# Attention and a gated feed-forward on one core: seven products joined in PSUM through a ScalarE copy, weights converted in pairs of chunks

## The chip, the core and the metric

The kernel runs on one NeuronCore of a Trainium2 chip. The metric is the device time of one execution, in microseconds (us), and lower is better. Four engines compute: PE (TensorE, matmuls, with PEld loading its weights), DVE (VectorE), ACT (ScalarE) and POOL (GpSimd). SP (SyncE) only issues DMAs here. Matmul results land in PSUM, which has eight banks; everything else lies in SBUF.

## What is computed

The reference, cut to what matters (8 batches, 8 heads, 576 positions, head size 64; 4608 tokens, model width 512, hidden width 2048):

```python
q_s = softmax(q, axis=-1)            # over the 64 of a head
k_s = softmax(k, axis=2)             # over the 576 positions
kv  = einsum('bhsd,bhse->bhde', k_s, v)
x   = einsum('bhsd,bhde->bhse', q_s, kv)   # as (4608, 512)
h   = x @ w_in                       # 512 -> 2048
g   = h * (1 / (1 + exp(-1.702 * h)))
out = g @ w_out                      # 2048 -> 512
```

The weights arrive as 64-bit floats and are turned into 32-bit ones on the chip.

## The kernel before, in words

**Precision.** Every large matmul is done three times on halves: a number is split into a rounded high part and the rest (`h` and `l`), and high x high, high x low and low x high are added in one PSUM bank.

**Work.** Tokens come in 12 tiles of 384. Tiles 0 and 1 go through the plain feed-forward: `g1` multiplies x by one of 16 chunks of `w_in` (12 matmuls of 384 columns), ACT applies the gelu, `g2` multiplies by the chunk of `w_out` (three times 3 matmuls of 512 columns). Tiles 2 to 11 go in five pairs, and there the first feed-forward matmul is Winograd's form of Strassen's scheme: a 2 x 2 block product made of seven products in place of eight. A pair takes eight cycles `n` (40 in all); a cycle has seven `product`s, numbered 1, 6, 2, 7, 5, 4, 3 in their order in the list `PROD` (6 matmuls of 384 columns each), and six `out_part`s, called G below, of the cycle before (6 matmuls of 512 columns each, into banks 0 to 5). With p1 to p7 the products, the four results are p1+p2, p1+p6+p7+p4, p1+p6+p7+p5 and p1+p6+p5+p3 (signs lie in the operands).

**Where the sums are made.** Products use banks 6 and 7. Before, p2, p4 and p3 join a bank that already holds a product (`JOINS`); the other sums are additions of a bank and an SBUF tile by DVE, in `add`: five per cycle. ACT copies p1 out and applies the gelu (`finish`), rounds its result to the high part, and DVE subtracts to get the low part.

**Attention.** For each batch: maximum over positions (`k_max`, DVE and a POOL reduction), subtraction and exp (`k_sub`), 40 small matmul pairs (`kv_pairs`), division. For each tile: the softmax of q (`q_soft`), transposes on PE (`q_tr`), the product with kv (`x_pairs`), copies out of PSUM (`x_raw`), sums and splits of x (`t_make`, `x_split`). For batches 0 and 1 and tiles 0 to 3 heads come in fours, later in twos.

**Weights.** A chunk is loaded (`load_w`, 512 KB), converted by two ACT and four DVE instructions (`conv_w`: of 512 elements per partition), and stored back to DRAM (`store`), from where the 40 cycles refill slots of SBUF. `s_make` forms the four weight sums of a cycle.

**Order.** Nothing is scheduled by a compiler here. `Plan` collects every step with an engine, an estimated cost, the buffers it reads and writes and a rank; `Plan.order` lets each engine take, whenever it is free, the ready step of lowest rank, and the instructions are issued in that order. So each engine runs a fixed sequence, in order, with semaphores between engines. `FIRST` is a table of ranks that replaces the written ranks of all steps below rank 16. Exp and gelu need different ACT tables, so ACT reloads a table between them.

Of the kernel before, what the change touches and what calls it, by code (L numbers as in the profile page):

```python
# [18 lines left out]
class Plan:  # L19
# [80 lines left out]

FIRST = [
# [20 lines left out]
]  # L122

# [11 lines left out]
def efficient_attention_then_gelu_ffn(  # L135
# [24 lines left out]
    LAG = 2  # L160
    SM = 512
# [54 lines left out]
    def early(tag, name, shape, batch):  # L216
        held[tag] = batch
        return sb(name, shape, tag=tag), (tag, 0)

    ek, ev, eq, en, etail = {}, {}, {}, {}, {}  # L220
    for gr in range(2):
        ek[0, gr] = early(f"wi{5 + gr}", f"ek0{gr}", [P, 4, CM, D], 0)
        eq[0, gr] = early(f"wi{7 + gr}", f"eq0{gr}", [P, 4, C, D], 0)
        en[0, gr] = early(f"wo{7 + gr}", f"en0{gr}", [P, C, 4, D], 0)
        en[1, gr] = early(f"wo{10 + gr}", f"en1{gr}", [P, C, 4, D], 1)
        ev[0, gr] = early(f"w{'io'[gr]}9", f"ev0{gr}", [P, 4, CM, D], 0)
        ek[1, gr] = early(f"wo{14 + gr}", f"ek1{gr}", [P, 4, CM, D], 1)
        eq[1, gr] = early(f"wi{14 + gr}", f"eq1{gr}", [P, 4, C, D], 1)
        ev[1, gr] = early(f"wo{12 + gr}", f"ev1{gr}", [P, 4, CM, D], 1)
    em, _ = early("wi13", "em", [P, 4 * 4 * D], 1)  # L230
    emx = [em[:, y * 4 * D : (y + 1) * 4 * D].rearrange("p (h d) -> p h d", h=4) for y in range(2)]
    em1 = em[:, 2 * 4 * D :]
    et, _ = early("wi10", "et", [P, H * (D + W)], 0)
# [10 lines left out]
        for kind in ("wi", "wo", "sh", "sl")  # L244
# [5 lines left out]

    def load_w(j, kind, rank):
        tag = f"{kind}{j}"

        def run():
            raw = sb(f"raw", [P, 2 * DM], I32, tag=tag)
            raws[tag] = raw
            if kind == "wi":
                nc.sync.dma_start(
                    out=raw.rearrange("p (c f) -> p c f", c=KC),
                    in_=w_in[:, 2 * j * P : 2 * (j + 1) * P].rearrange("(c p) f -> p c f", p=P),  # L260
                )
            else:
                nc.sync.dma_start(out=raw, in_=w_out[j * P : (j + 1) * P, :])

        plan.add("SP", plan.ISSUE, (), ((tag, 0), (tag, "v")), rank, run, size=2 * DM * 4 * P)

    nt = [0]

    def next_tmp():
        nt[0] += 1  # L270
        return nt[0] % 3

    def conv_w(j, kind, rank):
# [5 lines left out]
        tag = f"{kind}{j}"  # L279
        i = next_tmp()  # L280
        ff = tmp[i]
        f = ff.bitcast(I32)

        def words():
            return raws[tag].rearrange("p (f t) -> p f t", t=2)
# [8 lines left out]
        def c3():  # L294
            w = words()
            nc.vector.scalar_tensor_tensor(f, f, 3, w[:, :, 0], ALU.logical_shift_left, ALU.bitwise_or)  # L296
            nc.vector.scalar_tensor_tensor(f, w[:, :, 1], -0x80000000, f, ALU.bitwise_and, ALU.bitwise_or)

        def c5():
            w = sb("w", [P, 2 * DM], F32R, tag=tag)  # L300
            nc.scalar.copy(w[:, :DM], ff)
            raws[tag] = w

        def c6():
            w = raws[tag]
            wh, wl = w[:, :DM], w[:, DM:]
            nc.vector.tensor_tensor(out=wl, in0=ff, in1=wh.bitcast(F32), op=ALU.subtract)
            dst = wi if kind == "wi" else wo
            dst[0][j], dst[1][j] = (
                x.rearrange("p (c f) -> p c f", c=KC) if kind == "wi" else x for x in (wh, wl)  # L310
            )
# [925 lines left out]
```

## Time and profile before

| | us |
|---|---|
| median of 3 runs (lowest, highest) | 900.97 (899.77, 901.08) |
| the profiled execution, whole | 897.6 |
| its span, first to last instruction | 895.8 |
| PE busy | 852.4 (95%) |
| DVE busy | 561.4 (63%) |
| ACT busy | 482.1 (54%) |

The share of PE is an average over very different stretches: the first 83.6 us, in which weights and the first attention are made, the stretch to 224 us, in which tiles 0 and 1 are finished and the cycles start, and the 40 cycles. Matmuls overlap in PE's pipeline, so a matmul's own duration is longer than the step from its start to the next one's start; the step is what counts.

### The profile page before, as it was taken

What the parts mean: (1) busy time and instruction counts of PE and PEld (TensorE: products, weight loads), DVE (VectorE), ACT (ScalarE), POOL (GpSimd) and SP (SyncE); (2) the same over time, 40 slices, a digit from 0 to 9 for tenths busy, and PEclk for the clock granted to TensorE, in tenths of its full rate; (3) what the DMA queues carried; (4) which work ended last, traced back from release to release, by engine and by line L of the source; (5) the groups of instructions that cost most, each with busy time, mean ns of one, the idle gap of its engine ahead of it and who ended that gap; (6) DMA issues with size and microseconds to landing.
All of it is one profiled execution on the core that took longest, in us unless ns stands there. A gap on an engine that the chain in (4) does not pass through costs nothing.

```text
span 895.8 us, 13356 instructions
## 1 busy us (share of the span) xinstructions
PE 852.4 (95%) x4960; PEld 744.4 (83%) x4960; DVE 561.4 (63%) x1090; ACT 482.1 (54%) x856; POOL 29.8 (3%) x35
## 2 busy tenths in 40 slices
PE   3779999898999999899999999999999999999998
PEld 3668988687888888788898888789888889898896
DVE  8989989987977756647646646646553346332332
ACT  3776668877676447656635545525643326332222
POOL 1100000020200000101000001000000000000000
PEclk9889999999999999999999999999999999999999
DMA  9999974268565558957556648736744545745341
GB/s 277 281 318 399 375 229 134 102 174 222 181 206 198 196 200 252 279 183 241 174 177 232 214 171 249 233 135 211 253 161 166 198 153 190 268 162 216 140 153 70
DMA packets 133184, 187.52 MB, mean 209 GB/s; under 512 B 65536, under 2 KB 96256, under 8 KB 133120
## 3 DMA queue, kind: packets, MB, share of 16 engines
q1 hardware_dynamic: 133120, 186.68, 62.6%
q8 instruction: 39, 0.64, 0.3%
q14 instruction: 25, 0.20, 0.1%
HBM read 152.04 MB, written 34.60 MB: 208 GB/s over the span
## 4 chain that ended last, share of the span: by engine, by line
PE 83%; DVE 8%; DMA 4%; ACT 2%; SPq 1%; issue 1%; DVEq 0%; ACTq 0%
PE bank L1013 35%; PE bank L942 30%; PE bank L699 6%; PE bank L731 6%; PE bank L525 2%; DMA qt<-in_q 2%; PE bank L675 2%; DVE g L958 1%; PE bank L608 1%; DMA ev<-in_v 1%; DVE qm L587 1%; PE bank L670 1%; DVE tmp L296 1%; DMA raw<-in_moe_w_out 1%; DMA out<-tmp 1%
## 5 line engine op out<-in xcount | busy, mean ns | idle before, releaser
L1013 PE MATMUL bank<-w,gp 128*128 128x512 f32 x954 | 254.4, 396 | 0.6 <-ACT gp L969 0.4
L1013 PEld LDWEIGHTS bank<-w,gp 128*128 128x128 f32 x954 | 176.2, 188 | 36.6 <-issue 3.8
L942 PE MATMUL bank<-xc,w 128*128 128x384 f32 x960 | 190.6, 338 | 6.5 <-DVE g L958 4.5
L958 DVE TENSOR_TENSOR g<-bank,g 128x384 f32<-128x384 f32 x200 | 110.9, 556 | 127.2 <-PE bank L942 118.7
L942 PEld LDWEIGHTS bank<-xc,w 128*128 128x128 f32 x960 | 170.0, 188 | 18.3 <-DVE g L958 6.9
L942 PE MATMUL bank<-w 128*128 128x384 f32 x720 | 141.3, 340 | 4.2 <-DVE g L958 4.1
L966 ACT ACTIVATE g<-g 128x384 f32<-128x384 f32 x120 | 63.1, 526 | 146.4 <-DVE g L958 146.1
L942 PEld LDWEIGHTS bank<-w 128*128 128x128 f32 x720 | 128.6, 189 | 11.9 <-DVE g L958 6.0
L972 DVE TENSOR_TENSOR gp<-g,gp 128x384 fp32r<-128x384 f32 x106 | 58.6, 556 | 85.5 <-ACT gp L969 84.3
L1013 PE MATMUL bank<-w,gh 128*128 128x512 f32 x324 | 103.3, 400 | 0.0
L699 PE MATMUL bank<-xh,w 128*128 128x384 f32 x256 | 73.8, 351 | 4.1 <-ACT g L705 2.6
L966 ACT ACTIVATE g<-bank 128x384 f32<-128x384 f32 x40 | 19.7, 492 | 98.0 <-PE bank L942 97.9
L1013 PEld LDWEIGHTS bank<-w,gh 128*128 128x128 f32 x324 | 59.3, 188 | 12.1 <-issue 3.2
L1013 PE MATMUL bank<-w,gl 128*128 128x512 f32 x162 | 63.9, 395 | 0.0
L731 PE MATMUL bank<-w,gh 128*128 128x512 f32 x192 | 62.5, 407 | 0.2 <-ACT gh L708 0.2
L969 ACT CAST gp<-g 128x384 fp32r<-128x384 f32 x106 | 54.6, 515 | 3.4
L972 DVE TENSOR_TENSOR gl<-g,gh 128x384 fp32r<-128x384 f32 x54 | 30.0, 556 | 41.5 <-ACT gh L969 40.6
L699 PEld LDWEIGHTS bank<-xh,w 128*128 128x128 f32 x256 | 48.7, 196 | 6.7 <-ACT g L705 3.3
L699 PE MATMUL bank<-xl,w 128*128 128x384 f32 x128 | 44.3, 346 | 0.0
L731 PEld LDWEIGHTS bank<-w,gh 128*128 128x128 f32 x192 | 35.6, 190 | 7.9 <-issue 1.2
L731 PE MATMUL bank<-w,gl 128*128 128x512 f32 x96 | 38.7, 403 | 2.4 <-DVE gl L711 2.4
L463 POOL PARTITION_ALL_REDUCE mx<-mx x24 | 23.9, 997 | 501.8 <-DVE mx L459 501.8
(123 smaller groups left out, 995.8 us busy)
## 6 DMA issues: line engine op xcount, KB each, us to landing
w<-dwo SPq DMA_DIRECT2D x80, 512.0 KB, 4.9
w<-dwi SPq DMA_DIRECT2D x44, 512.0 KB, 3.9
w<-dsh SPq DMA_DIRECT2D x32, 512.0 KB, 6.2
w<-dsl SPq DMA_DIRECT2D x32, 512.0 KB, 7.2
out<-tmp SPq DMA_DIRECT2D x36, 256.0 KB, 3.3
raw<-in_moe_w_out SPq DMA_DIRECT2D x16, 512.0 KB, 9.0
raw<-in_moe_w_in SPq DMA_DIRECT2D x16, 512.0 KB, 10.1
dwi<-w SPq DMA_DIRECT2D x16, 512.0 KB, 6.6
```

The costliest lines, as they stand in the source:

```text
L296: nc.vector.scalar_tensor_tensor(f, f, 3, w[:, :, 0], ALU.logical_shift_left, ALU.bitwise_or)
L463: nc.gpsimd.partition_all_reduce(flat, flat, P, bass_isa.ReduceOp.max)
L525: nc.tensor.matmul(pk[r0 : r0 + D, m, cols], lhs, rhs, start=c == 0, stop=c == CM, tile_position=(0, r0))
L675: nc.tensor.matmul(po[ro], kx[ri, ro], qx[ri], start=True, stop=True, tile_position=((a ^ odd) * D, a * D))
L699: nc.tensor.matmul(ph, wi[w][j][:, c, :], x[:, c, :], start=c == 0 and i == 0, stop=c == KC - 1 and i == 2,)
L731: nc.tensor.matmul(po[c], x[:, cs], wo[w][j], start=j == 0 and i == 0, stop=j == NJ - 1 and i == 2)
L942: nc.tensor.matmul(pb, ws[w][:, c * P : (c + 1) * P], xx[x][:, c * TB : (c + 1) * TB], start=p not in JOINS and c == 0 and i == 0, stop=c ...
L958: lambda: nc.vector.tensor_tensor(out=d, in0=pb, in1=o, op=ALU.add),
L966: lambda: nc.scalar.activation(d, src, AF.Gelu_apprx_sigmoid), table="gelu")
L969: plan.add("ACT", act(TB), (dk,), hk, early_, lambda: nc.scalar.copy(get()[0], d))
L972: lambda: nc.vector.tensor_tensor(out=get()[1], in0=d, in1=get()[0].bitcast(F32), op=ALU.subtract),
L1013: nc.tensor.matmul(po, x[:, cs], w[:, h * DM : (h + 1) * DM], start=m == 0 and e == 0 and i == 0, stop=m == NQ - 1 and e == 1 and i == 2,)
```

## The change

1. **Sums in PSUM.** After p1, ACT copies bank 6 into bank 7 (`keep`), and p6, p7 and p4 join bank 7, p2 joins bank 6, p3 joins p5 in bank 6; only p1 and p5 start a bank (`FRESH`). ACT copies bank 7 out after p6 and after p7. DVE keeps two additions per cycle of five. A matmul joins only where an earlier matmul has written the bank; after `x_pairs` has used bank 7 (`seeded`), one extra matmul of 384 columns into bank 7 goes ahead of p1.
2. **Cycle.** `CYCLE` has a new order of products and G, and two slots for attention; `q_tr` uses bank 6; the copies out of its bank, and all of `x_raw`, go to DVE for tiles 4 and later, and so does kv's division. `gate` makes ACT's attention exps wait for a point late in a cycle's products.
3. **Pairs of chunks.** Chunks 2 to 15 are loaded and converted two at a time, with instructions of 1024 elements. Four of the `w_in` sums are stored as they are converted (`dsr`) and loaded by `s_make`, instead of being added again.
4. **Fours.** Heads come in fours everywhere.
5. **Ranks.** `FIRST` covers every step below rank 48, and holds other numbers.

```diff
+LIMIT = 48
 FIRST = [
-    10880, -13523, -14348, -9747, -11942, -16592, -13346, -10333, -12197, -7632, -8889, -7141, -10712, -8175, -8834,
...
+    -7413, -6848, -6096, -5820, -6089, -6938, -5819, -4545, -5036, -4544, -4855, 7784, -5658, 8215, 7935, -5883,
...
-        plan.add("ACT", 0.66, (R,), (T,), rank, c1)
-        plan.add("DVE", 0.40, (R,), (R,), rank, c2)
-        plan.add("DVE", 1.36, (R, T), (T,), rank, c3)
-        plan.add("ACT", 0.62, (T,), (R,), rank, c5)
-        plan.add("DVE", 0.69, (R, T), ((tag, 1),), rank, c6)
+        T, R = ("work", i), [(tag, 0) for tag in tags]
+        m = n * DM
+        plan.add("ACT", 0.23 + m / 1190, R, (T,), rank, c1)
+        plan.add("DVE", 0.13 + m / 1900, R, R, rank, c2)
+        plan.add("DVE", 0.147 + m / 960, (*R, T), (T,), rank, c3)
+        plan.add("DVE", 0.147 + m / 960, (*R, T), (T,), rank, c4)
+        plan.add("ACT", act(m), (T,), R, rank, c5)
+        plan.add("DVE", 0.157 + m / 960, (*R, T), [(tag, 1) for tag in tags], rank, c6)
...
     def group(b):
-        return 4 if b < 2 else 2
+        return 4
...
-            nc.scalar.copy(qT, pq[:, :TB])
-
-        plan.add("ACT", act(TB), (PB,), (Q,), rank, run_c)
+            (nc.vector.tensor_copy if t >= EARLY_T else nc.scalar.copy)(qT, pq[:, :TB])
+
+        plan.add("DVE" if t >= EARLY_T else "ACT", act(TB), (PB,), (Q,), rank, run_c)
...
     BANK = {1: 6, 2: 6, 5: 6, 3: 6, 6: 7, 7: 7, 4: 7}
-    JOINS = (2, 4, 3)
+    FRESH = (1, 5)
...
+            if seed:
+                nc.tensor.matmul(bank[7][:, :TB], ws[0][:, :P], xx[0][:, :TB], start=True, stop=True)
...
-                        start=p not in JOINS and c == 0 and i == 0, stop=c == 1 and i == 2,
+                        start=p in FRESH and c == 0 and i == 0, stop=c == 1 and i == 2,
...
+        def keep(dst, key):
+            plan.add("ACT", act(TB), (PB,), (key,), early_, lambda: nc.scalar.copy(dst, pb))
+
         if p == 1:
-            st["p1"] = d, dk = temp()
-            plan.add("ACT", act(TB), (PB,), (dk,), early_, lambda: nc.scalar.copy(d, pb))
-        elif p == 6:
-            st["u2"] = temp()
-            add(st["u2"], st["p1"])
-        elif p == 2:
-            finish(pb, (PB,), temp(), 0, 0)
-        elif p == 7:
-            st["u3"] = temp()
-            add(st["u3"], st["u2"])
-        elif p == 5:
-            add(st["u3"], st["u3"])
-            finish(st["u3"][0], (st["u3"][1],), st["u3"], 1, 1)
-        elif p == 4:
-            c21 = temp()
-            add(c21, st["u2"])
-            finish(c21[0], (c21[1],), c21, 1, 0)
+            keep(bank[7][:, :TB], ("bank", 7))
+        elif p in (6, 7):
+            st[p] = temp()
+            keep(*st[p])
+        elif p in (2, 4):
+            finish(pb, (PB,), temp(), int(p == 4), 0)
         else:
-            c12 = temp()
-            add(c12, st["u2"])
-            finish(c12[0], (c12[1],), c12, 0, 1)
+            dst = st[7] if p == 5 else temp()
+            add(dst, st[7 if p == 5 else 6])
+            finish(dst[0], (dst[1],), dst, int(p == 5), 1)
...
-    CYCLE = [1, ("G", 0), 6, ("G", 1), 2, "early", ("G", 2), "wide", ("G", 3), 7, ("G", 4), 5, 4, ("G", 5), 3, "tail"]
+    CYCLE = [1, ("G", 0), 6, 2, ("G", 1), 7, 5, ("G", 2), 4, 3, ("G", 3), "slot0", ("G", 4), "slot1", ("G", 5)]
```

How the order of the instructions moves, at three places. First PE in a late cycle without attention. Lines L942 and L1102 are products (bank_69 and bank_70 are banks 6 and 7; `xc` and `w` are the slots of x, `xc` for products 1, 6, 2, 7), L1013 and L1167 are G. Before:

```order
L942 MATMUL bank_70<-xc,w 128x384 x6
L942 MATMUL bank_69<-xc,w 128x384 x6
L1013 MATMUL bank_63<-w,gp 128x512 x6
L1013 MATMUL bank_64<-w,gp 128x512 x6
L942 MATMUL bank_69<-xc,w 128x384 x6
L1013 MATMUL bank_65<-w,gp 128x512 x6
L1013 MATMUL bank_66<-w,gp 128x512 x6
L942 MATMUL bank_70<-xc,w 128x384 x6
L1013 MATMUL bank_67<-w,gp 128x512 x6
L942 MATMUL bank_69<-w 128x384 x6
L942 MATMUL bank_70<-w 128x384 x6
L1013 MATMUL bank_68<-w,gp 128x512 x6
```

And with the change:

```order
L1102 MATMUL bank_69<-xc,w 128x384 x6
L1167 MATMUL bank_63<-w,gp 128x512 x6
L1102 MATMUL bank_70<-xc,w 128x384 x6
L1102 MATMUL bank_69<-xc,w 128x384 x6
L1167 MATMUL bank_64<-w,gp 128x512 x6
L1102 MATMUL bank_70<-xc,w 128x384 x6
L1102 MATMUL bank_69<-w 128x384 x6
L1167 MATMUL bank_65<-w,gp 128x512 x6
L1102 MATMUL bank_70<-w 128x384 x6
L1102 MATMUL bank_69<-w 128x384 x6
```

Before, p6 stood ahead of p1 and two G stood between the first products; now p1 comes first, one G stands between it and p6, and three G follow p3.

Second, ACT in the same cycle, from the copy after p1 on. Before (L977 copies p1, L966 is the gelu, L969 the rounding):

```order
L977 COPY g_84<-bank_69 128x384
L966 ACTIVATE g_78<-bank_69 128x384
L969 CAST gp<-g_78 128x384
L966 ACTIVATE g_79<-g_79 128x384
L969 CAST gp<-g_79 128x384
L966 ACTIVATE g_80<-g_80 128x384
L969 CAST gp<-g_80 128x384
L966 ACTIVATE g_81<-g_81 128x384
L969 CAST gp<-g_81 128x384
```

And with the change (L1138 is `keep`):

```order
L1138 COPY bank_70<-bank_69 128x384
L1138 COPY work_83<-bank_70 128x384
L1127 ACTIVATE work_84<-bank_69 128x384
L1131 CAST gh_89<-work_84 128x384
L1138 COPY work_84<-bank_70 128x384
L1127 ACTIVATE work_84<-work_84 128x384
L1131 CAST gp<-work_84 128x384
L1127 ACTIVATE g_78<-bank_70 128x384
L1131 CAST gp<-g_78 128x384
L1127 ACTIVATE g_79<-g_79 128x384
L1131 CAST gp<-g_79 128x384
```

One copy of a cycle became three, and the first of them writes the bank that p6 joins.

Third, the head of SP's queue of DMAs. Before:

```order
L428 DMA eq_132<-in_q 128x4x192
L345 DMA et<-in_k 64x8x64
L360 DMA ek_131<-in_k 128x4x256
L428 DMA eq_140<-in_q 128x4x192
L374 DMA ev_143<-in_v 128x4x256
L360 DMA ek_139<-in_k 128x4x256
L345 DMA kl_115<-in_k 64x8x64
L374 DMA ev_135<-in_v 128x4x256
L348 DMA et<-in_v 64x8x64
```

And with the change:

```order
L508 DMA eq_120<-in_q 128x4x192
L433 DMA ek_119<-in_k 128x4x256
L418 DMA et<-in_k 64x8x64
L433 DMA ek_119<-in_k 128x4x256
L447 DMA ev_124<-in_v 128x4x256
L508 DMA eq_123<-in_q 64x4x192 x2
L314 DMA raw<-in_moe_w_in 128x4x256 x2
L421 DMA et<-in_v 64x8x64
L508 DMA eq_120<-in_q 128x4x192
L418 DMA kl_105<-in_k 64x8x64
L447 DMA ev_121<-in_v 128x4x256
```

Two chunks of `w_in`, values of batch 1 (`ev_124`) and queries of tile 1 (`eq_123`) now stand ahead of the values of batch 0 (`ev_121`; before `ev_135` and `ev_143`), for which PE's first matmul waits.

## Rows read from the trace of the kernel before

**Rows 1.** The page: busy time of the engines, and two in 40 slices.

```profile
PE 852.4 (95%) x4960; PEld 744.4 (83%) x4960; DVE 561.4 (63%) x1090; ACT 482.1 (54%) x856; POOL 29.8 (3%) x35
PE   3779999898999999899999999999999999999998
DVE  8989989987977756647646646646553346332332
```

**Rows 2.** Busy time by stretch, five stretches; the first row names the columns.

```profile
core 0: us, PE busy (x) PEld busy (x) DVE busy (x) ACT busy (x) POOL busy (x), PEclk, DMA share, GB/s
0.00:68.00 68.00, 43.62 (x438) 37.74 (x439) 59.65 (x116) 42.20 (x75) 5.90 (x11) 0.91 0.99 293
68.00:83.60 15.60, 15.22 (x73) 13.46 (x71) 15.19 (x28) 9.99 (x19) 0.00 (x0) 0.95 1.05 394
83.60:224.00 140.40, 133.30 (x798) 115.52 (x798) 124.43 (x242) 107.64 (x185) 8.92 (x10) 0.99 0.67 215
224.00:868.00 644.00, 636.45 (x3544) 557.31 (x3543) 354.02 (x694) 314.98 (x565) 15.01 (x15) 1.00 0.59 200
868.00:895.80 27.80, 23.82 (x113) 20.32 (x112) 8.08 (x14) 7.31 (x14) 0.00 (x0) 1.00 0.23 88
```

**Rows 3.** Timeline of PE: its first matmul, the ninth g1, the first cycle's end.

```profile
14.32 1.12 PE L525 MATMUL bank<-ev,ek 128*64 128x64 f32 x16 [14.32 <-DMA ev<-in_v]
...
83.62 0.44 PE L699 MATMUL bank<-xh,w 128*128 128x384 f32 x1
...
223.95 2.25 PE L942 MATMUL bank<-xc,w 128*128 128x384 f32 x12
```

**Rows 4.** Lines of DVE in 0:224: the conversions, and one of 1024 elements.

```profile
L296 DVE SCALAR_TENSOR_TENSOR tmp<-tmp,raw 128x512 int32<-128x512 int32 x32 | 22.5, 702 | 1.5 <-ACT tmp L288 0.3
L307 DVE TENSOR_TENSOR w<-tmp,w 128x512 fp32r<-128x512 f32 x32 | 21.5, 686 | 0.3 <-ACT w L301 0.2
L292 DVE TENSOR_SCALAR raw<-raw 128x512 uint32<-128x512 uint32 x32 | 13.2, 422 | 1.4 <-DMA raw<-in_moe_w_out 1.4
L478 DVE TENSOR_TENSOR ek<-ek,em 128x1024 f32<-128x1024 f32 x4 | 4.9, 1218 | 0.0
```

**Rows 5.** What PE waited for from 224 us on: total, times, longest.

```profile
PE bank L942 <- DVE g L958: 5.4, 10, 1.0
PE bank L942 <- DVE raw L629: 1.4, 1, 1.4
PE bank L1013 <- ACT gp L969: 0.4, 1, 0.4
PE bank L1013 <- DVE gp L972: 0.2, 1, 0.2
```

**Rows 6.** Timeline of PE in a late cycle without attention.

```profile
860.67 1.21 PE L942 MATMUL bank<-xc,w 128*128 128x384 f32 x6
861.72 1.55 PE L1013 MATMUL bank<-w,gp 128*128 128x512 f32 x6
863.11 1.22 PE L942 MATMUL bank<-w 128*128 128x384 f32 x6
...
867.66 2.25 PE L942 MATMUL bank<-xc,w 128*128 128x384 f32 x12
869.76 2.89 PE L1013 MATMUL bank<-w,gp 128*128 128x512 f32 x12
```

**Rows 7.** Timeline of ACT: the copy of p1 there, and a table load elsewhere.

```profile
404.70 0.47 ACT L615 COPY qT<-bank 128x384 f32<-128x384 f32 x1
405.19 1.28 ACT L583 ACT_TABLE_LOAD   x1
406.48 0.53 ACT L583 ACTIVATE qt<-qt 128x384 f32<-128x384 f32 x1
...
869.96 0.48 ACT L977 COPY g<-bank 128x384 f32<-128x384 f32 x1 [0.43 <-PE bank L942]
```

**Rows 8.** Lines of the page: DVE's additions and ACT's gelu on their results.

```profile
L958 DVE TENSOR_TENSOR g<-bank,g 128x384 f32<-128x384 f32 x200 | 110.9, 556 | 127.2 <-PE bank L942 118.7
L966 ACT ACTIVATE g<-g 128x384 f32<-128x384 f32 x120 | 63.1, 526 | 146.4 <-DVE g L958 146.1
```

More of the change, by code (lines that the diff above doesn't have):

```diff
@@ L32, in add @@
         deps = set()
+        for b in writes:
+            if (a := self.alias.get(b)) and b not in self.writer:
+                deps.update((self.writer[a], *self.readers.get(a, ())))
         for b in reads:
@@ L296, in c3, with c4, halves @@
             nc.vector.scalar_tensor_tensor(f, f, 3, w[:, :, 0], ALU.logical_shift_left, ALU.bitwise_or)
+        def c4():
+            w = words()
             nc.vector.scalar_tensor_tensor(f, w[:, :, 1], -0x80000000, f, ALU.bitwise_and, ALU.bitwise_or)
+        def halves():
+            return ff.rearrange("p (j f) -> p j f", j=n)
         def c5():
-            w = sb("w", [P, 2 * DM], F32R, tag=tag)
-            nc.scalar.copy(w[:, :DM], ff)
-            raws[tag] = w
-        def c6():
[L305 to L311, printed above, removed]
@@ L320, in bc, with run_d @@
+        plan.add("ACT", act(m), (T,), R, rank, c5)
+        plan.add("DVE", 0.157 + m / 960, (*R, T), [(tag, 1) for tag in tags], rank, c6)
+        if kind == "wi" and j >= SPILL:
+            def run_d():
+                nc.sync.dma_start(out=dw[f"sr{j // 2}"], in_=work[i])
+            plan.add("SP", plan.ISSUE, (T,), (("dw", f"sr{j // 2}"),), rank, run_d, size=2 * DM * 4 * P)
     def bc(a, n):
@@ L405, in load_q @@
         n = qgroup(t)
-        alloc = ()
+        alloc, after = (), ()
         if t < 2:
@@ L437, in load_q @@
         plan.add(
-            "SP", plan.ISSUE * len(parts(t)) * len(runs), behind(1 < t < EARLY_T), (key, *alloc), rank, run,
+            "SP", plan.ISSUE * len(parts(t)) * len(runs), behind(1 < t < EARLY_T) + after, (key, *alloc), rank, run,
             size=n * TB * D * 4,
@@ L487, in k_sub @@
         L = (lkey, i)
-        plan.add("DVE", dve(n * CM * D) + dve(n * D), (key, M, lkey, *((("wi13", "v"),) if b < 2 else ())), (key, L), rank, run)
-        plan.add("ACT", act(n * CM * D) + act(n * D), (key, L), (key, L), rank, run_exp, table="exp")
+        plan.add("DVE", dve(n * CM * D), (key, M), (key,), rank, run)
+        plan.add("DVE", dve(n * D), (M, lkey), (L,), rank, run_tail)
+        gate = () if gate is None else (("gate", gate),)
+        plan.add("ACT", act(n * CM * D) + act(n * D), (key, L, *gate), (key, L), rank, run_exp, table="exp")
     ng = [0]
@@ L633, in x_raw @@
         old = [("x", 0, "hl"[t % 2], y) for y in range(NP)] if t < EARLY_T else []
-        plan.add("DVE" if hp % 2 else "ACT", act(TB), (PB,), (("raw", t % 2, hp), *old), rank, run)
+        plan.add("DVE" if hp % 2 or t >= EARLY_T else "ACT", act(TB), (PB,), (("raw", t % 2, hp), *old), rank, run)
     def x_out(t, hp, px, PB, rank):
@@ L846, in run @@
             if s == 1:
-                tt[which] = sb(f"t{which}", [P, 2, TB], tag=GTAG[which - 1])
+                if which not in tt:
+                    two = sb("tw", [P, 2, 2 * DM], tag=GTAG[which - 1])
+                    for y in range(2):
+                        tt[which + y] = two[:, y, : 2 * TB].rearrange("p (k f) -> p k f", k=2)
             elif 0 not in tt:
@@ L865, in t_make @@
         old = [("x", 1, h, y) for h in "hl" for y in range(NP)] if s == 2 else []
+        if s == 1 and which % 2:
+            old = both(GTAG[which])
+        elif s == 1:
+            reads = (*reads, *tkeys(s, which - 1)[:1])
         plan.add("DVE", dve(2 * TB), reads, (*tkeys(s, which), *old), rank, run)
@@ L890, in run_l @@
             nc.vector.tensor_tensor(out=make(tl), in0=src(), in1=raws[th].bitcast(F32)[:, : 2 * TB], op=ALU.subtract)
-        plan.add("ACT", act(2 * TB), reads, both(th), rank, run_h)
+        plan.add("ACT", act(2 * TB), reads, both(th) + (both(tl) if s == 1 and th in ("wo2", "wo4", "wo6") else ()), rank, run_h)
         plan.add("DVE", dve(2 * TB), (*reads, *both(th)), both(tl), rank, run_l)
@@ L935, in weights @@
             return [raws[tag][:, i * HM : (i + 1) * HM] for tag in (sh, sl)]
+        seed = p == 1 and state.pop("lost", False)
         def run():
@@ L948, in product @@
         wkeys = both({1: ev, 2: ev, 4: od}[p]) if p in (1, 2, 4) else (*both(sh), *both(sl))
-        plan.add("PE", 1.045, (*wkeys, *both(xh_), *both(xl_)), (PB,), rank, run)
+        clear = (("bank", 7),) if seed else ()
+        plan.add("PE", 1.22 if seed else 1.045, (*wkeys, *both(xh_), *both(xl_)), (PB, *clear), rank, run)
         early_ = rank - 12
@@ L966, in finish @@
                      lambda: nc.scalar.activation(d, src, AF.Gelu_apprx_sigmoid), table="gelu")
-            i, get, (hk, lk) = pair()
+            i, get, (hk, lk), fresh, after = pair()
             gof[n, e, col] = get, hk + lk
-            plan.add("ACT", act(TB), (dk,), hk, early_, lambda: nc.scalar.copy(get()[0], d))
+            gate = (("gate", n),) if (e, col) == (1, 0) else ()
+            plan.add("ACT", act(TB), (dk, *after), (*hk, *fresh, *gate), early_, lambda: nc.scalar.copy(get()[0], d))
             plan.add(
@@ L1061, in efficient_attention_then_gelu_ffn @@
         at(-86 + i, load_v, 0, i)
-    for j in range(NJ):
+    for j in (0, *range(1, NJ)):
+        if j > 1 and j % 2:
+            continue
         r = -84 if j < 1 else -70 + j
```

383 lines of the change are left out of this document (248 added, 135 removed), and 72 rows, old and new, of the table FIRST.

## The prediction

> **What bounds the kernel now.** I read the page first. PE is busy for 852.4 of 895.8 us [rows 1], so a gain can only come from PE's other 43 us, from stretches in which PE runs at a lower clock, or from less work on PE. In the 40 slices the reader should see that PE falls under 9 tenths at the left end, where DVE stands at 8 or 9, and that DVE falls to 6 or less on the right, where PE is full: DVE can only be the bound on the left.
>
> Then the busy time by stretch [rows 2]. PE is idle for 24.4 us in 0:68, for 0.4 in 68:83.6, for 7.1 in 83.6:224, for 7.5 in 224:868 and for 4.0 behind that. Of the first, 14.3 lie ahead of PE's first matmul, which waits for a DMA [rows 3]; the 4.0 at the end are the last copies and the store. [...] DMA is full in 0:68 (0.99). From 224 us on PE's waits [rows 5] make 7.4 of those 7.5 us: nearly all for DVE's additions (L958) or its copies, none longer than 1.4.
>
> In a clean cycle nothing is lost. Six product matmuls step on by 861.72 - 860.67 = 1.05 us, six of G by 863.11 - 861.72 = 1.39 [rows 6], so a cycle is 7 x 1.05 + 6 x 1.39 = 15.7 us, and none of the change's parts makes that less.
>
> **The seed: work added on PE.** The order has 16 extra matmuls of 384 columns, one after every second half of an `x_pairs`. At 1.05 / 6 = 0.175 us each they cost 2.8 us, on PE itself, so nothing covers them: **+2.8**.
>
> **The cycles, from 224 us on.** Three of DVE's five additions per cycle go (120 of 200, at 0.556 us [rows 8], 67 us of DVE); DVE takes over 48 copies out of PSUM of the same size and kv's division. ACT gains two copies per cycle, at the 0.48 us of the copy of p1 [rows 7], and loses copies, the divisions and 12 table loads. Both engines end with less work than before and neither is near PE's load, so their sums cost nothing; what matters is what is late in a cycle:
>
> - p6 now waits for ACT's copy of p1 into its bank; before, p6 could even stand ahead of p1. No row shows ACT writing PSUM. The nearest is the copy of p1 into SBUF: it starts 0.20 us after the G behind p1 (869.96 against 869.76) and takes 0.48 [rows 6, 7]. With some 0.05 to wake PE that is 0.73, and the cover is that G of 1.39. I take 0; if ACT is busy when p1 ends, everything over 0.66 us is paid.
> - p7 and p4 join a bank after ACT has copied it, with p2 or p5 (1.05) as the least cover, again against 0.73: 0.
> - p3 joins the bank that DVE's addition reads after p5: 0.20 + 0.556 + 0.05 = 0.81 against p4's 1.05. In 27 of 40 cycles a G stands in between as well; in 13 none does, and there only 0.24 us are left. What stands ahead of an addition on DVE is now larger (768 or 1024 elements instead of 384 or 512), up to 1.2 us [rows 4].
> - The exps of attention wait for the gate, so ACT meets them after p4's result; their result is wanted only a cycle later. What is queued behind them on ACT is p3's gelu and the next copy of p1, so that is the wait to watch.
> - Loads of keys and queries are issued a whole cycle ahead of their use, so the 1.4 us wait behind `raw` should go.
>
> Of 7.4 us of waits I expect 4 to be left, since DVE is freer but the slack in those 13 cycles is thin: **-3.4**. The bounds are 0 left and 12 (0.3 us in each of 40 cycles).
>
> **The start, up to 224 us.** Ahead of the 43rd product matmul, which began at 223.95 [rows 3], the order puts 28 single conversions fewer on DVE and 14 double ones more. A single one is 0.422 + 2 x 0.70 + 0.686 = 2.51 us [rows 4]. For the double one, no row has these operations at 1024 elements; a plain two-operand operation goes from 0.686 to 1.218, so I add 0.53 to each (1.23, twice, and 1.22) and 0.27 to the 0.422, whose cost per element is about half: 4.37. So 28 x 2.51 - 14 x 4.37 = 9.1 us of DVE go. With fours instead of twos I count 10.3 in all: 213.1 becomes 202.8, each the order's DVE instructions up to the one that matmul waits for, at the mean of its kind. Rows overlap a little, so 213.1 stands for 199.3 us of busy DVE [rows 2], and 202.8 for 189.6. With the same 24.7 us of idle DVE, DVE allows the 43rd product at 214.3.
>
> [...]
>
> PE allows it only later. From the ninth g1 at 83.62 [rows 3] to 224 PE was busy for 133.3 us [rows 2]; less 1.4 for the clock, 131.9. The change moves 18 matmuls of G (0.232 us each, 4.2 us) ahead of that point and 0.4 us behind it: 135.7. If the ninth g1 starts when it did, the 43rd product starts at 219.3, with PE as the bound and DVE 5 us ahead; I add 0.5 for a wait left over. Before, the same work would have been done at 224 + 3.8 = 227.8. So **-8.0**.
>
> That the ninth g1 starts when it did is my choice: DVE's sum up to what it waits for is 74.3 us before and 73.6 now, though the first g1 needs 36.3 in place of 25.3, since more is converted ahead of it. Against it: SP's queue puts 1.45 MB more ahead of PE's first matmul, 4.9 us at the 293 GB/s of the first stretch [rows 2]; that matmul moves to about 19, which costs nothing as long as PE is not what is late there (24.4 us idle in 0:68). For it: a search over these ranks may fill those gaps better. Bounds: 5 us either way.
>
> **The sum.** -8.0 - 3.4 + 2.8 = -8.6. The profiled execution took 897.6 us with a span of 895.8; the median of the runs is 901.0, 3.4 above it. I expect 889.0 by the first and so **892.4** by the second.
>
> **Rivals.**
>
> *All waits go.* Nothing left of 7.4 us, nothing of 8.5 before 224, and the first stretch 5 us shorter: -8.5 - 7.4 - 5 + 2.8 = -18.1, so 883. For it: DVE has 13 us less ahead of the products by the order's own sums; against it: the thin slack in 13 cycles. 0.20.
>
> *The start gives nothing.* DMA is full in the first stretch, pairs need both halves landed, and the values come 4.9 us later. Then 5 to 8 us of the gain are lost: 897.4 to 900.4. 0.13.
>
> *Joins wait in the crowded cycles.* In the 13 cycles without a G between p5 and p4, a DVE operation of attention in the way costs 0.6 more each: 8 us, 900.4. 0.05.
>
> *Slower: ACT's copy of p1 is late.* Place: p6, in each cycle with attention on ACT. An exp of 768 or 1024 elements and two table loads of 1.28 [rows 7] may stand between p4's result and the copy, with p3's gelu and rounding between them; when two exps fall into one cycle, they overrun the three G. PE cannot go past p6, its queue being in order. The gain is gone where the mean loss reaches 8.6 / 40 = 0.22 us a cycle; at 0.5 us in 31 cycles it is 15.5, and the kernel takes 908. Against it: before, ACT did as much around these points, and PE waited for ACT 0.4 us in all from 224 us on [rows 5]. 0.12.
>
> *Slower still: a table load costs more than its row.* In the rows the load takes 1.28 us and the next instruction starts 0.01 later (405.19 + 1.28 = 406.47, against 406.48) [rows 7]. If a switch took twice that, each of about 26 windows with an exp would be 2.6 us longer, some 1.9 over its slack: 49 us, 941. [...] 0.02.
>
> **How the numbers follow.** My forecast has 0.48, with a range of its own of 887 to 897 (2 to 8 us of waits left in the cycles, a little either way at the start). The range 884 to 902 adds the start that gives nothing, the crowded cycles and most of the case without waits, and leaves out the two slower cases. A measurement of this kernel can tell some 0.2% from no change, 1.8 us: under 899.2 is faster, over 902.8 slower. Faster takes the forecast, the case without waits and 0.10 of the start's: 0.78. Same takes the rest of that and the crowded cycles: 0.08. Slower takes the two last: 0.14.
>
> **What the changed kernel's profile would show.** If I am right, PE's idle time between the ninth g1 and the 43rd product is under 1 us and the 43rd product starts near 220; the late cycles still last 15.7 us; PE's waits from there on sum to some 4 us, on DVE's additions, with hardly any on ACT's copy into bank 7; the 16 seeds show 0.175 us each. I am wrong if PE waits for that copy in most cycles, if the ninth g1 starts after 89, or if waits after 220 exceed 8 us.

## The result, and the profile after

The changed kernel takes 873.6 us (median of four runs, 873.2 to 874.9), the kernel before 900.4 beside it: a ratio of 0.972, 95% interval 0.970 to 0.975. I had forecast 892.4 with a range of 884 to 902. It is faster, as forecast, but three times as much as I said. The profiled execution took 874.0 us with a span of 872.2, that of before 897.6 with 895.8: 23.6 us went between these two. In two of the runs below, those without the searched ranks, one execution of four and two of ten took 1.9 to 2.4 times as long as the others, and medians and comparisons leave these out.

The page of the changed kernel, busy time and slices, against [rows 1]:

```profile
PE 841.7 (96%) x4976; PEld 742.6 (85%) x4976; DVE 495.6 (57%) x828; ACT 453.4 (52%) x744; POOL 27.6 (3%) x23
PE   1789999999999999999999999999999999999998
DVE  9889979998666475543457534657342444312212
```

PE is full from the fourth slice on; in [rows 1] it dipped in the eighth, tenth and seventeenth. VectorE has 66 us less to do. PE's busy time fell by 10.7 us although 16 matmuls were added. That is the first sign that busy time is not work, and it is where my sum broke. The stretches, cut at the same events as [rows 2] (68 us, the ninth g1, the 43rd product, the last cycle's start), in the same columns:

```profile
0.00:68.00 68.00, 41.23 (x433) 35.90 (x433) 58.32 (x108) 34.26 (x51) 9.21 (x11) 0.95 0.95 303
68.00:81.86 13.86, 13.86 (x76) 13.12 (x75) 13.38 (x16) 10.23 (x16) 0.00 (x0) 1.00 1.02 407
81.86:215.50 133.64, 133.64 (x816) 117.71 (x816) 119.42 (x179) 88.44 (x129) 8.51 (x4) 1.00 0.66 224
215.50:844.20 628.70, 628.70 (x3544) 555.15 (x3542) 299.16 (x519) 313.19 (x535) 9.88 (x8) 1.00 0.65 211
844.20:872.20 28.00, 24.23 (x115) 20.69 (x113) 5.33 (x9) 7.27 (x14) 0.00 (x0) 1.00 0.26 94
```

PE is never idle from 68 us to the last cycle, and the granted clock is 1.00 there. The events themselves, from PE's timeline, against [rows 3]:

```profile
18.34 0.91 PE L615 MATMUL bank<-ev,ek 128*64 128x64 f32 x12 [18.34 <-DMA ev<-in_v]
...
81.92 0.34 PE L821 MATMUL bank<-xh,w 128*128 128x384 f32 x1
...
215.45 1.21 PE L1102 MATMUL bank<-xc,w 128*128 128x384 f32 x6
```

The first matmul came 4 us later and cost nothing, the ninth g1 1.7 us earlier, the 43rd product 8.5 earlier. With the 3.8 us of G that moved ahead of it, the same work was done 12.3 us sooner. From there to the end it was 671.9 us and is 656.7; less the 3.8 and with the seeds' 2.8, PE lost 14.1 us less there. So 12.3 + 14.1 - 2.8 = 23.6: the whole difference.

The two parts are not equally firm. In eleven other traces of kernels whose start is that of the changed kernel the ninth g1 began between 79.8 and 85.8 us, so its 1.7 us here is scatter (in a second trace of the changed kernel it began at 83.5). But in all twelve the 43rd product began 133.5 us after it, where the kernel before would have taken 140.3 + 3.8 for the same work: 10.6 us are gained there in every trace.

**Where 14.1 us can go, when PE's waits showed 7.4.** A stop of the kernel before, that is a place where PE may not start its next matmul, on the engines' timeline:

```profile
256.45 0.49 PE L608 MATMUL bank<-ident,qt 128*128 128x128 f32 x3
256.65 0.56 DVE L958 TENSOR_TENSOR g<-bank,g 128x384 f32<-128x384 f32 x1 [1.25 <-PE bank L942]
...
257.26 0.82 PEld L942 LDWEIGHTS bank<-xc,w 128*128 128x128 f32 x5 [0.56 <-DVE g L958]
257.26 0.97 PE L942 MATMUL bank<-xc,w 128*128 128x384 f32 x4 [0.32 <-DVE g L958]
```

Three transposes stand between p3 and the next p1. They are issued in 0.25 us (the rows of their weight loads end at 256.70), so p1 could have started at 256.70. It opens bank 6, which VectorE is still adding up, and starts at 257.26: 0.56 us lost. PE's row calls 0.32 of it idle, because the row of the last transpose ends at 256.94; the row of the weight load (PEld) has the full 0.56. And the four matmuls behind it span 0.97 where four elsewhere span 0.88: some 0.1 more after each stop. So the waits to read are those of the weight loads. Theirs in the kernel before, from the 43rd product on (us in total, times, longest):

```profile
PEld bank L942 <- DVE g L958: 9.2, 14, 1.3
PEld bank L1013 <- issue: 7.1, 15, 0.6
PEld bank L675 <- issue: 2.2, 6, 0.4
PEld bank L942 <- DVE raw L629: 2.1, 1, 2.1
PEld bank L525 <- ACT qT L615: 1.5, 4, 0.4
...
PEld bank L1013 <- ACT gp L969: 0.8, 1, 0.8
PEld bank L1013 <- DVE gp L972: 0.6, 1, 0.6
```

and in the changed kernel:

```profile
PEld bank L1167 <- issue: 7.4, 15, 0.6
PEld bank L797 <- DVE gp L1134: 1.5, 4, 0.4
PEld bank L797 <- issue: 1.4, 4, 0.4
PEld bank L615 <- issue: 1.1, 3, 0.4
...
PEld bank L797 <- DVE kl L569: 0.7, 2, 0.4
```

All rows of the first view sum to 27.3 us, of the second to 15.0. What both have (0.4 or 0.6 each, around the small matmuls of attention) is no loss that a change here can take; what is gone is the waits of products for VectorE and ScalarE. From the ninth g1 to the 43rd product the same view sums to 13.1 before, where PE showed 7.1 idle, and to 2.8 after. A second measure agrees: each step from one matmul's start to the next, less the steady step of its kind (0.174 us for a product, 0.2335 for G), leaves 15.4 us lost before from the 43rd product on and 1.7 after. Below, "lost in the cycles" is that measure.

### The profile page after: what moved, and what is told of

It is laid out like the page before. It is cut to its first block, busy times and chain, and to the rows that moved or that the text cites. A ratio compares the mean times of both kernels' runs of the same rounds, so it can differ in the third digit from the quotient of the medians.

```text
span 872.2 us, 12905 instructions
## 1 busy us (share of the span) xinstructions
PE 841.7 (96%) x4976; PEld 742.6 (85%) x4976; DVE 495.6 (57%) x828; ACT 453.4 (52%) x744; POOL 27.6 (3%) x23
## 4 chain that ended last, share of the span: by engine, by line
PE 96%; SPq 1%; DMA 1%; DVE 1%; ACT 1%; POOL 0%; issue 0%; ACTq 0%
PE bank L1167 39%; PE bank L1102 34%; PE bank L853 8%; PE bank L821 7%; PE bank L615 3%; PE bank L730 2%; PE bank L797 2%; PE bank L792 1%; DMA ev<-in_v 1%; SPq L508 0%; ACT ek L572 0%; PE bank L1099 0%; POOL mx L548 0%; SPq L418 0%; SPq L421 0%
## 5 line engine op out<-in xcount | busy, mean ns | idle before, releaser
L1102 PE MATMUL bank<-xc,w 128*128 128x384 f32 x960 | 183.6, 336 | 0.0
L1102 PEld LDWEIGHTS bank<-xc,w 128*128 128x128 f32 x960 | 170.1, 188 | 7.7
L1167 PE MATMUL bank<-w,gp 128*128 128x512 f32 x630 | 170.8, 396 | 0.0
L1167 PEld LDWEIGHTS bank<-w,gp 128*128 128x128 f32 x630 | 115.8, 188 | 24.3 <-issue 3.6
L1102 PE MATMUL bank<-w 128*128 128x384 f32 x720 | 136.1, 336 | 0.0
L1102 PEld LDWEIGHTS bank<-w 128*128 128x128 f32 x720 | 126.7, 188 | 2.7
L1167 PE MATMUL bank<-w,gh 128*128 128x512 f32 x324 | 103.6, 401 | 0.0
L1167 PE MATMUL bank<-w 128*128 128x512 f32 x324 | 93.0, 395 | 0.0
L1138 ACT COPY bank<-bank 128x384 f32<-128x384 f32 x40 | 18.5, 463 | 115.5 <-PE bank L1102 115.5
L1167 PEld LDWEIGHTS bank<-w 128*128 128x128 f32 x324 | 59.8, 188 | 11.8 <-issue 0.6
L1167 PEld LDWEIGHTS bank<-w,gh 128*128 128x128 f32 x324 | 58.8, 188 | 12.0 <-issue 3.2
L1167 PE MATMUL bank<-w,gl 128*128 128x512 f32 x162 | 64.0, 395 | 0.0
L1138 ACT COPY g<-bank 128x384 f32<-128x384 f32 x40 | 19.2, 479 | 48.6 <-PE bank L1102 48.5
L1138 ACT COPY work<-bank 128x384 f32<-128x384 f32 x40 | 19.2, 479 | 48.2 <-PE bank L1102 48.1
L1134 DVE TENSOR_TENSOR gp<-work,gp 128x384 fp32r<-128x384 f32 x35 | 19.3, 555 | 37.0 <-ACT gp L1131 37.0
L1134 DVE TENSOR_TENSOR gp<-g,gp 128x384 fp32r<-128x384 f32 x35 | 19.7, 562 | 35.1 <-ACT gp L1131 35.1
```

Source lines behind the costliest of these rows:

```text
L1102: nc.tensor.matmul(pb, ws[w][:, c * P : (c + 1) * P], xx[x][:, c * TB : (c + 1) * TB], start=p in FRESH and c == 0 and i == 0, stop=c == 1 ...
L1134: lambda: nc.vector.tensor_tensor(out=get()[1], in0=d, in1=get()[0].bitcast(F32), op=ALU.subtract),
L1138: plan.add("ACT", act(TB), (PB,), (key,), early_, lambda: nc.scalar.copy(dst, pb))
L1167: nc.tensor.matmul(po, x[:, cs], w[:, h * DM : (h + 1) * DM], start=m == 0 and e == 0 and i == 0, stop=m == NQ - 1 and e == 1 and i == 2,)
```

## The experiments

Ranks and cycles of the first five cycles are kept in all runs that edit the cycle, so that the searched ranks keep their steps; "35 cycles" are the others.

**The order alone, in the kernel before.**

```diff
-    CYCLE = [1, ("G", 0), 6, ("G", 1), 2, "early", ("G", 2), "wide", ("G", 3), 7, ("G", 4), 5, 4, ("G", 5), 3, "tail"]
+    CYCLE = [1, ("G", 0), 6, 2, "early", ("G", 1), "wide", ("G", 2), 7, ("G", 3), 5, 4, ("G", 4), 3, "tail", ("G", 5)]
```

> The kernel before, with its written cycle alone changed: p2 follows p6 and the last G stands behind p3 and the transposes, so that p1 finds its bank added up. Joins, conversions and heads stay as they were. Theory P: most of the losses at p1 (9.5 us by PE's start-to-start steps) go, 890 to 893 us. Theory J: within 3 us of the kernel before, 898 to 903 us.

891.8 us (ratio 0.993, 0.990 to 0.996), 7.5 us less than the kernel before beside it. In the traces 5.1 us of the gain lie from the 43rd product on (666.7 in place of 671.9) and 1.8 ahead of it: of the 14.1 us the order alone gives 5.1. The seven stops of the kind shown above (5.2 us) are gone. Eight others are there, of 0.2 to 1.2 us each: five at an addition that stood behind VectorE's steps of attention, one at VectorE's copy of attention's result, two at ScalarE's copy of p1 (0.73 each).

**The old joins in the changed kernel.** In 35 cycles p6, p7 and p4 are added on VectorE as before.

```diff
+        fresh_ = (1, 6, 7, 5) if old else FRESH
...
+        if old:
+            if p == 1:
+                st["p1"] = temp()
+                keep(*st["p1"])
...
+                dst = temp()
+                add(dst, st[{6: "p1", 7: "u2", 4: "u2", 3: "u2"}[p]])
...
```

> The changed kernel with the old joins in 35 of 40 cycles: p1 is copied to SBUF, p6 and p7 open their bank, and p6, p7 and p4 are added on VectorE as before; the written cycle, its slots and the seeds (now without use) stay. Theory J: most of the 14 us that PE lost in the cycles of the kernel before comes back, 882 to 886 us. Theory P: the cover decides, so within 2 us of the changed kernel, 872 to 876 us. Theory L (VectorE's load): 67 us more of VectorE work in 640 make some additions late, 875 to 880 us.

877.1 us (873.9 to 879.3). Lost in the cycles: 2.8 in place of 1.7. VectorE was busy for 353 us in 214:840 in place of 299, and it did not matter. The joins in PSUM, which give the change its name, are worth about 1 us by themselves in this cycle.

**Strictly in the written cycle.** PE's steps from the sixth cycle on get one more common key, so that they run in the order of their ranks.

```diff
+        if engine == "PE" and rank >= 61:
+            writes = (*writes, "seq")
```

> From the sixth cycle on PE's instructions follow the written cycle strictly; in the changed kernel the planner moves a G here and there. Both theories: every hand-over still has a G or two products over it, so the time stays at 872 to 875 us, and the start-to-start steps of PE show no step longer than usual. If it is slower by more than 3 us, the planner's moves of G were part of the gain.

891.1 us: 17 us slower, against the expectation. The waits of the weight loads there (L732 are transposes, L1101 seeds, L799 `x_pairs`):

```profile
PEld bank L732 <- DVE raw L753: 7.5, 3, 3.5
...
PEld bank L1101 <- DVE raw L753: 5.1, 4, 1.6
PEld bank L799 <- DVE qT L739: 3.0, 1, 3.0
```

Transposes, `x_pairs` and seeds stand where they are written even if VectorE still copies what they wait for. In the changed kernel the planner often pulls G 0 and 1 of the next cycle ahead of its p1 and G 2 ahead of p6. The cycle of PE is not fixed, and it may not be: it is an order with G in reserve.

**Two hand-overs with nothing over them,** on top of the strict order, each in 35 cycles (`CYCLE` itself stays for the others): p6 directly behind p1, the first `CYCLE2`; and three G ahead of p3, so that p3's bank is wanted at once, the second.

```diff
+    CYCLE2 = [1, 6, ("G", 0), 2, ("G", 1), 7, 5, ("G", 2), 4, 3, ("G", 3), "slot0", ("G", 4), "slot1", ("G", 5)]
...
+    CYCLE2 = [1, ("G", 0), 6, 2, ("G", 1), 7, 5, ("G", 2), 4, ("G", 3), ("G", 4), ("G", 5), 3, "slot0", "slot1"]
...
```

> The same strict order, but p6 stands directly behind p1 in 35 of 40 cycles, so nothing covers ScalarE's copy of p1 into bank 7. It prices that hand-over: my estimate of 0.73 us a cycle (0.20 to start, 0.48 to copy, 0.05 to wake PE) gives +26 us, 899 us; if ScalarE's write to PSUM were as dear as twice its row it would be +42 us.

919.8 us, 28.7 over the strict order alone. The 35 stops at p6 lost some 27 us by PE's steps, 0.72 in 33 of them (I had estimated 0.73) and 1.42 in two, and the matmul behind each stop another 0.11. The two views of the same 35 waits, PE's and the weight loads':

```profile
PE bank L1104 <- ACT bank L1140: 20.8, 35, 1.3
...
PEld bank L1104 <- ACT bank L1140: 32.0, 35, 1.6
```

31.2 us were lost from start to start: PE's row shows two thirds of it.

> The same strict order, but three G stand ahead of p3 instead of behind it, so that p1 of the next cycle, or a transpose or x_pairs in between, follows p3 on bank 6 with nothing over p3's addition on VectorE. Theory P (places: the losses of the kernel before were hand-overs of a bank with nothing over them): 0.8 us at each of 35 boundaries and as much again where a transpose stands there, +28 to +60 us, 902 to 934 us. Theory J (joins: the losses came from the additions that p6, p7 and p4 needed): p3 and its addition are as before, so under +10 us.

987.4 us, 96 over the strict order alone and beyond what either theory gave. One hand-over from p3 through VectorE to p1 (p3's last matmul is issued by 931.62):

```profile
930.57 1.21 PE L1104 MATMUL bank<-w 128*128 128x384 f32 x6
931.82 0.56 DVE L1121 TENSOR_TENSOR g<-bank,work 128x384 f32<-128x384 f32 x1 [3.60 <-PE bank L1104]
932.43 0.81 PE L1104 MATMUL bank<-xc,w 128*128 128x384 f32 x3 [0.65 <-DVE g L1121]
```

0.81 us, as I had worked it out for p3's addition. Where attention stands between p3 and p1, hand-overs follow one another: a transpose waits for p3's addition, and what comes behind it for VectorE's copy of its result. At the eight p1 behind transposes 1.7 to 5.8 us were lost between p3 and p1, by PE's steps.

A part is neither theory's: the clock. From 214 to 820 us the granted clock fell to 0.50 ten times, each time behind such stops, for 51 us in all, and steps that waited for nothing took longer there, 19 us more in all. In the changed kernel it is 1.00 over these cycles. The mean, one such stretch, and six G in it, which take 2.56 from start to start in place of 1.39:

```profile
214.32:820.00 605.68, 537.94 (x2938) 463.85 (x2937) 267.86 (x462) 260.71 (x435) 10.04 (x8) 0.96 0.57 183
508.30:515.10 6.80, 6.09 (x17) 5.11 (x18) 2.03 (x4) 1.22 (x3) 0.00 (x0) 0.50 0.65 201
...
512.00 2.76 PE L1169 MATMUL bank<-w,gp 128*128 128x512 f32 x6
```

The 0.81 us above was taken where it was 1.00.

**The old written places, then all of them together.** In the changed kernel, without the strict order, G goes back to where the cycle of before had it; then with the old joins too.

```diff
+    CYCLE2 = [1, ("G", 0), 6, ("G", 1), 2, ("G", 2), ("G", 3), 7, ("G", 4), 5, 4, ("G", 5), 3, "slot0", "slot1"]
...
```

> The changed kernel with the G of 35 of 40 cycles written where the cycle of before had them (behind p1, p6, p2, p2, p7 and p4), so that p3, the transposes and the next p1 stand together as then; the planner may still move a G. Joins in PSUM stay. Theory P (written places): a good part of the 12 us that the cycles gained is lost again, 880 to 886 us. If the planner puts a G between p3 and p1 by itself, the written places are not what matters either, and it stays at 872 to 876 us.

880.5 us, lost in the cycles 6.9: 5 us of the 14 come back.

> The same with the old joins too, so that of the cycles only the heads in fours, the loads a cycle ahead and the slots on bank 6 are left of the change. Theory P and J together: the 12 us are back, 884 to 890 us. If it stays under 878 us, the losses of the kernel before came from what is left: where the transposes stood (bank 7, straight ahead of p1) and what attention put in the way.

879.3 us, lost 7.1: the joins add nothing to it. So 8 us had another source, and the next runs put attention's steps back to the start of their cycle, without the gate: alone, with the old joins, and with the old joins and places.

```diff
-            at(base(n + i + 1) + 2.9, lambda rank, i=i: k_sub(b, i, rank, n + i + 1 if n >= 0 else None))
+            at(base(n + i + 1) + (1 if n >= 3 else 2.9), lambda rank, i=i: k_sub(b, i, rank, n + i + 1 if 0 <= n < 3 else None))
...
-        at(base(n + 1) + 2.9, lambda rank: q_soft(t, i, (rank, rank, rank, *((n + 1,) if n >= 0 else ()))))
+        at(base(n + 1) + (0.5 if n >= 3 else 2.9), lambda rank: q_soft(t, i, (rank, rank, rank, *((n + 1,) if 0 <= n < 3 else ()))))
```

> The changed kernel with attention's steps (softmax of queries, subtraction and exp of keys) from the fourth cycle on ranked at the start of their cycle in place of its end, and without the gate. Joins and cycle stay. Theory A with joins in PSUM: the copies of p1, p6 and p7 on ScalarE stand behind exps at times, +3 to +8 us over the changed kernel. If the covers are wide enough, under +1.5 us.

879.2 us, lost 5.5.

> The same with the old joins on VectorE in 35 cycles. Theory A: the additions of p6, p7 and p4 stand behind attention's steps, +6 to +12 us over the changed kernel, most of what was lost before. If joins and attention's place do not matter together either, within 3 us.

878.2 us, lost 4.4.

> The same with the old joins and the old written places of G: attention early, joins on VectorE, G as before. Theory A and P together: the 13.7 us are back, +10 to +14 us over the changed kernel. If it stays at +6 or less, as with the cycle and the joins alone, the rest came from the heads in fours or from the transposes on bank 6 in place of 7.

893.2 us, lost 15.5, and 2.9 more at transposes behind `x_pairs`, which the measure leaves out. That is no less than in the kernel before, but not at the same places: there 13.5 us were lost ahead of products, here 1.4 ahead of products and 11.0 ahead of `x_pairs` and transposes, for p3's addition and VectorE's copies. One stretch of the lower clock behind a stop took 1.4 of it.

> The changed kernel itself, unchanged, on the same chip as the other three: 873 to 875 us.

875.0 us, on the same chip as the last three, and lost 1.7 again. The weight loads' longest waits with everything undone (L797 are `x_pairs`, L730 transposes, L1122 additions):

```profile
PEld bank L797 <- DVE g L1122: 5.8, 5, 1.8
...
PEld bank L730 <- DVE raw L751: 3.8, 2, 2.7
PEld bank L797 <- DVE qT L737: 3.6, 6, 1.8
```

From the 43rd product to the end the changed kernel takes 656.7 us; with the old places 661.7, with the old joins 657.8, with attention early 661.5; with joins and places 662.1, with joins and attention 660.4; with all three 673.1. Places and attention together without the joins were not tried, nor the transposes back on bank 7, nor heads in twos. Each costs 1 to 5 us alone, all three 16 (18 by the medians): the reading that fits is that they draw on the same reserve: a late addition hurts only if nothing covers it, and it is late only if attention or more additions are in the way.

**The start: the conversions.** The first try issues each double conversion as two instructions of 512; the second adds half a subtraction, 0.6 us, behind each double one.

```diff
-            nc.vector.tensor_scalar(lo, lo, 29, None, ALU.logical_shift_right)
+            for y in range(n):
+                lo = words(y)[:, :, 0].bitcast(U32)
+                nc.vector.tensor_scalar(lo, lo, 29, None, ALU.logical_shift_right)
...
+            if n > 1:
+                nc.vector.tensor_tensor(out=w[:, 0, 1], in0=ff[:, :DM], in1=w[:, 0, 0].bitcast(F32), op=ALU.subtract)
```

> The changed kernel with each double conversion issued as two instructions of 512 elements in place of one of 1024, in the same place of the plan; loads, tiles and everything else stay. VectorE gets 14 x (2 x 2.51 - 4.35) = 9.4 us more work, ScalarE some 5. If VectorE sets the pace up to the 43rd product matmul, that matmul moves from 215.5 to about 224 and the time to 881 us. If PE sets it, with VectorE 5 us ahead as I reckoned, 873 to 878 us. If neither does there, no change.

874.7 us (872.4 to 878.1): nothing. But this was no fair undoing. VectorE's busy time up to 215 us, in the changed kernel and in this one:

```profile
sum 215.00, PE 188.22 PEld 166.32 DVE 190.62 ACT 132.92 POOL 17.72; mean PE 188.22 PEld 166.32 DVE 190.62 ACT 132.92 POOL 17.72
```

```profile
sum 215.00, PE 189.15 PEld 167.68 DVE 193.97 ACT 135.71 POOL 17.71; mean PE 189.15 PEld 167.68 DVE 193.97 ACT 135.71 POOL 17.71
```

Only 3.4 us more, not 9.4: two halves that do not need one another overlap, two rows of 0.69 in 1.29 (last section).

> The changed kernel with 0.6 us more VectorE work behind each double conversion (half of the last subtraction is done twice), 14 x 0.6 = 8.4 us in all: by VectorE's time the undoing of the double conversions, which the run with two instructions side by side was not, since their steps overlapped and VectorE had only 3 us more to do. If VectorE sets the pace up to the 43rd product, 879 to 883 us; if it has 5 us to spare there, 873 to 878 us; if it has more than 8, no change.

877.5 us (875.2 to 879.1), 2.4 and 3.8 us over the two medians of the changed kernel; the 43rd product came at 218.2, with the first matmul 1.6 us later than in the changed kernel. So of some 8 us of VectorE's time about a third reached the end, near what "5 us to spare" gave. Of the 2.7 us by which the 43rd product is later, 1.2 is the ninth g1's scatter; the 135.1 us between the two, where the other traces have 133.5, are clear of it. 1.2 more were lost behind the 43rd product.

**The start: the search.**

> The changed kernel without the searched ranks: all steps keep the ranks that the program writes. If the search only fills small gaps, +2 to +6 us, 875 to 880 us; if the start's gain is the search's, the gain of 8 to 12 us up to the 43rd product goes, 882 to 890 us.

881.5 us, 6.5 and 7.9 us over the two medians of the changed kernel. The ninth g1 comes at 86.8 and the 43rd product at 219.4, with 12 matmuls of G fewer ahead of it; with their 2.8 us it would be 222.2, 6.8 later than in the changed kernel's trace. The cycles lose 1.9 us, as with the search.

> The kernel before without its searched ranks (313 of its first steps). Beside the run without ranks on the changed kernel it tells what the search was worth in each: if equally much, the difference of the two stays near 27 us and the start's gain is the conversions' and the heads'; if the two come within 18 us, a third of the gain is the search's.

900.6 us, ratio 1.0005 (0.998 to 1.003): in the kernel before, the search was worth nothing that can be measured. The two runs without it stand 19.1 us apart, between the two cases of the expectation. So some 7 of the 27 us, about a quarter, are the search over more steps, and they lie before the 43rd product. What else went from the start beside conversions and search (heads in fours, larger loads) was not tried apart, so a part of the start's gain has no run that isolates it.

**Fewer seeds.** In the 14 later cycles that need a seed, p1 goes to SBUF, p6 opens the bank, and VectorE adds p1 three times.

```diff
+        if wide and p in (1, 6, 7, 4):
+            st[p] = temp()
+            if p == 1:
+                keep(*st[p])
+            else:
+                add(st[p], st[1])
...
```

> The changed kernel without 14 of its 16 seeds: in a cycle that would need one, p1 is copied to SBUF, p6 opens bank 7 anew, and VectorE adds p1 to p6, p7 and p4. If a seed costs what its row shows (0.175 us, with nothing over it) and the three additions stay covered, -2.5 us, 870 to 872 us. If the additions come late, 0.3 us in each of 14 cycles, it is even or slower.

871.3 us (870.6 to 874.2), ratio to the kernel before 0.970 (0.968 to 0.972). It beats the kernel before; against the changed kernel (873.6 and 875.0, in other runs) the intervals touch. Of the 2.5 us saved on PE the profile keeps 1.0 from the 43rd product on (655.7 us against 656.7), since 1.5 more are lost to late additions. The rest of the difference is the start's scatter.

## Why the prediction was wrong

- **What bounds the kernel now: wrong by half.** "From 224 us on PE's waits make 7.4 of those 7.5 us" reads idle time between rows that are drawn past the next start (a product's row lasts 0.34 us, its step 0.174). The weight loads' waits in the same trace, which I did not read, show products waiting for VectorE for 9.2 + 2.1 us where PE's rows show 5.4 + 1.4; by PE's steps 15.4 us were lost.
- **The cycles, the step that failed: "of 7.4 us of waits I expect 4 to be left: -3.4".** Measured: -14.1. The loss to take was twice what I read, and what was left of PE's waits is 0, not 4. I expected waits at p3's addition in 13 crowded cycles; the changed kernel has p5 and p4 without a G between in 15, and lost nothing there. I never looked at what actually stood in those waits: seven p1 behind transposes behind p3. Nor did I price the place of attention's steps, beyond the exps' gate, or the G that the planner has in reserve.
- **The start: direction right, size short.** -8.0 was forecast, -12.3 measured, 10.6 of it behind the ninth g1. The 135.7 us of PE's work from the ninth g1 on contained stops that its busy time hides; the same work took 133.5. No run shows the 1.4 us taken off for the clock in that sum: in the trace of before the granted clock was 0.50 for 3.4 us of this stretch (219.9 to 223.3), behind a stop, and PE's steps lost 1.6 there, six product matmuls taking 2.08 in place of 1.05; in the changed kernel's trace it was 1.00 throughout. The 0.5 for a wait left over did not come, and the ninth g1 was 1.7 early, which is scatter and within the 5 either way that I gave. That the search would do this much was a half-sentence.
- **VectorE at the start: right, and of little weight.** The double conversion is 4.35 us by its rows against my 4.37, and VectorE was busy for 191.1 us up to 215.5 against 189.6:

```profile
L355 DVE SCALAR_TENSOR_TENSOR work<-work,raw 128x1024 int32<-128x1024 int32 x14 | 17.1, 1223 | 1.4 <-ACT work L347 1.0
L359 DVE SCALAR_TENSOR_TENSOR work<-raw,work 128x1024 int32<-128x1024 int32 x14 | 17.1, 1221 | 0.3
L376 DVE TENSOR_TENSOR w<-work,w 128x1024 fp32r<-128x1024 f32 x14 | 17.1, 1220 | 2.6 <-ACT w L366 2.6
L351 DVE TENSOR_SCALAR raw<-raw 128x1024 uint32<-128x1024 uint32 x14 | 9.6, 689 | 0.0
```

- **The seeds: right.** 16 at 0.176 us by PE's steps, 2.8.
- **ScalarE's copy into the bank: right.** Its row is 0.463 us, against 0.48 taken:

```profile
L1138 ACT COPY bank<-bank x40: 463/463/472, 194.8 to 845.5; 128x384 f32<-128x384 f32 x40
```

In the last cycle it starts at 845.45, 0.20 behind p1's end at 845.25, as [rows 6, 7] gave. PE never waits for it; with nothing over it, it would have cost 0.72 + 0.11 a cycle, which is what the rival "slower" needed. That rival, and the one of dearer table loads, did not come: in the changed kernel's trace 58 table loads take 1.283 us each, and in 56 of them the next instruction starts 0.01 later.
- **The clean cycle: right.** Seven cycles to the last one took 844.2 - 734.8 = 109.4, 15.6 each.
- **"All waits go"** happened, but for the 5 us of its first stretch, of which 1.7 came, and I gave it 0.20. Its 883 was worked out with the same 7.4, so even the right case had the wrong price, and the range ended at 884.

## What to carry to other kernels

Read what TensorE loses from its weight loads' waits, or from start to start, never from the idle time between matmul rows (7.4 us in the kernel before, where the steps show 15.4); and before pricing a cure, list the places of the stops. A share of busy time is not a floor: PE's busy time shrank here from 852.4 to 841.7 us while 16 matmuls were added. Slack looks shared: three undoings that cost 1 to 5 us alone cost 16 to 18 together, so measure them together too; and an order held strictly lost 17 us that the planner, with six G a cycle to move, had covered.

## What was not expected of the hardware

- A stop costs more than its length: the second matmul behind it starts some 0.11 us late (4.0 us behind 35 stops in the run with p6 behind p1).
- Rows on VectorE overlap. An operation of 512 elements has a row of 0.69 us, but one that does not need the one ahead starts 0.60 behind its start; one that does, 0.73. Two such halves take 1.29 on the timeline of the first run on the conversions, where one of 1024 elements takes 1.22, so an instruction less saves some 0.07 us between neighbours of this kind and, as I estimate it, some 0.2 in a chain (two steps of 0.73 less one of 1.22 and its gap of 0.04), not the 0.15 that the rows give (0.686 at 512 elements, less the 0.53 for 512 more). The timeline of the two halves:

```profile
90.92 0.76 DVE L358 TENSOR_SCALAR raw<-raw 128x512 uint32<-128x512 uint32 x2
91.59 1.29 DVE L363 SCALAR_TENSOR_TENSOR work<-work,raw 128x512 int32<-128x512 int32 x2
```

- ScalarE writes 384 elements to PSUM in 0.463 us, a little faster than to SBUF (0.480, the other copies of that line).
